# FFN1 over two groups of weight chunks that stay on chip, plain products for one tile pair, and a new order of parts

## The chip, the cores and the metric

The kernel runs on one core of a Trainium2 chip. The metric is the device time of one execution in microseconds. Engines are named as in the profile: PE is TensorE's matmuls and PEld its weight loads, DVE is VectorE, ACT is ScalarE, POOL is GpSimd, SP is SyncE, whose queue issues nearly all DMAs here.

## What is computed

The block takes x (2048 tokens, 512 features), normalizes each token, and computes two branches of the normalized xn. All arithmetic is float32.

```python
xn  = layernorm(x)
q, k, v = split(xn @ wqkv)                     # 32 heads of 16
pq, pk  = q @ w_phi, k @ w_phi                 # per head, 16 x 16
phi = concat(softmax(p), softmax(-p))          # 32 features a head
kv  = phi_k^T v ;  z = sum over tokens of phi_k
o   = (phi_q kv) / (phi_q z + 1e-6)
s   = o @ wo
h   = xn @ w1 + b1                             # 512 -> 1792
g   = silu( mish(h) @ w2 )                     # 1792 -> 512
out = x + s * g
```

## The kernel before, in words

**Tiles.** Tokens are cut into 16 tiles of 128 (t = 0 to 15), the 1792 hidden features into 7 chunks of 256 (b = 0 to 6). A float32 product is made of three products of a high and a low part (`mm3`, line 422): low times high, high times low, high times high. The parts come from `split` (line 442): ACT writes the rounded high part, DVE or POOL subtracts it from the source to give the low part. w_phi is folded into the weights of q and k on chip (`folded`, line 482).

**Fewer products by sums.** k and v of two tiles t and t + 4 are made together by a scheme of seven block products in the place of eight (`kv_a` to `kv_d`, lines 622 to 656). It takes sums and differences of the blocks of the normalized x (`sums_x`, line 545: tiles ts, their parts th and tl) and of the weights (`weights_s`, line 903: four sums ws, their parts in the tile wss). A pair takes 42 products 512 wide where plain ones would take 48. FFN1 uses the same scheme (`ffn1a` to `ffn1d`, lines 812 to 840) on 1024 tokens (half q = 0 or 1) and one chunk b at a time; n = 7q + b counts these units, 0 to 13.

**Parts of the work.** norm (N) loads a tile, normalizes and transposes it and writes its two parts to DRAM (scr), the sums to scrT. q_proj (Q) makes q and parks it in DRAM (qd); q_soft (S) brings it back and makes the softmaxes. kv_acc (A) adds a pair to kv and z; `sums` (z, line 922) finishes them: kvf is written to kvd in DRAM and read back as kvw, which the numerators (num, U, PSUM tiles pn) need. den (D) divides, att_out (O) multiplies with wo. FFN1 brings its half of x back from scr and scrT by `load_g` (L, line 774): 14 transfers of 512 KB into tiles fb0 to fb2 and ft0 to ft3, high and low. `prep1` (P, line 745) loads a chunk of w1, makes its sums and splits it into four tiles (w1ah, w1al, w1sh, w1sl), and writes these to DRAM as w1d; for the second half `again1` (M, line 761) loads the four back as w1b. The hidden values go to DRAM (hd); ffn2 (G, line 842) loads them, applies Mish and multiplies with w2; final (E) applies Silu, multiplies by the attention branch and adds x.

**What sets the order.** The functions only record operations (`Program.call`, line 107). TensorE executes the parts in the order of the table ORDER (line 36), one token a part: Ka0 is `kv_a(0)`, Fa3 is `ffn1a(3)`. For the other engines `Program.simulate` (line 177) plays the program with estimated costs and due times and takes at each point the most urgent operation that is ready; operations written with `either` or `copy` go to whichever of two engines is free. Each engine then executes its list strictly in order, and waits at an instruction whose inputs are missing. SP's queue is one of these lists. Every operation is recorded by line 345, so the profile's groups are told apart by tiles. On chip lie 38 large buffers of 4 KB a partition (`SLOTS`, line 33): one holds a part of a w1 chunk, an fb or ft tile, a normalized tile, and so on; PSUM has 8 banks.

Of the kernel before, what the change touches and what calls it, by code (L numbers as in the profile page):

```python
# [17 lines left out]
P = 128  # L18
# [10 lines left out]
BACK, COLD, DRATE, LANES, SWITCH = 1500, 3400, 300, 8, 300  # L29
# [19 lines left out]
class Op:  # L49
    __slots__ = ("impl", "reads", "writes", "at", "idx", "succ", "ndep", "late", "new", "ready", "start", "eng", "sets", "slack", "open", "soon", "pos", "deps", "lock", "part", "half", "code", "tiles")  # L50


class Program:


    def __init__(self, nc):
        self.eng = {"PE": nc.tensor, "V": nc.vector, "G": nc.gpsimd, "A": nc.scalar, "Q": nc.sync}
        self.ops, self.tag, self.cap, self.pe = [], {}, {}, []
        self.group, self.slack, self.part, self.half = None, SLACK, None, False
# [87 lines left out]
    def links(self):  # L147
# [20 lines left out]
        for o in ops:  # L168
            o.new = []
            o.tiles = {n[0] for n in o.reads | o.writes if n[0] in self.tag}  # L170
            for n in o.tiles:
                self.uses[n] = self.uses.get(n, 0) + 1
                if n not in self.first:
                    self.first[n] = o
                    o.new.append(n)

    def simulate(self, at):
# [15 lines left out]
        free = dict(self.cap)  # L193
# [5 lines left out]
        half = False  # L199
        dma = port = 0  # L200
# [24 lines left out]

        def go(o, e):
            nonlocal aset, dma, port, half, code, fetched
# [23 lines left out]
            for n in o.new:  # L251
                free[self.tag[n]] -= 1
                want[self.tag[n]].remove(n)
            busy[e] = now + dur
            end = now + dur + (200 if e == "PE" else 140)
            if e == "Q":
# [5 lines left out]
                end = max(dma + 1000, now + 2000 + nb / 200)  # L262
# [121 lines left out]
def block_kernel(ctx: ExitStack, tc: tile.TileContext, x, wqkT, wv, phi, wo, w1, b1, w2, out):  # L384
# [124 lines left out]
    scr = [dram.tile([P, 4, 2, KC, P], F32, name=f"scr{g}") for g in range(NG)]  # L509
# [9 lines left out]
    def norm(t):  # L519
# [21 lines left out]
        Q.dma_start(scr[g][:, i], f32(w))  # L541
# [79 lines left out]

    def kv_a(p):
# [46 lines left out]
    def kv_acc(p):  # L669
# [8 lines left out]
        with one():  # L678
# [6 lines left out]
            prog.halves()  # L685
# [22 lines left out]
    def num(n):  # L708
# [3 lines left out]
        with one():  # L712
# [8 lines left out]
            prog.halves()  # L721
# [23 lines left out]
    def prep1(b):  # L745
# [26 lines left out]
    hd, w1d, part = {}, {}, {}  # L772

    def load_g(q):

        def combo(name, src):
            ts = [slot([P, 4, 2, P], f"f{name}{'hl'[u]}{q}", F32R) for u in range(2)]
# [4 lines left out]
        fx[q] = [combo(f"b{n}", lambda u: scr[2 * q + g][:, :, u, 2 * k:2 * k + 2]) for n, g, k in ((0, 0, 0), (1, 0, 1), (2, 1, 1))]  # L782
        fx[q] += [combo(f"t{n}", lambda u: scrT[q][:, :, u, n]) for n in range(4)]
# [101 lines left out]
    w["kv"] = [None] * 7  # L885
    kr, vr, sr = [None] * 2, [None] * 2, [None] * 4

    def weights_k(i):
# [6 lines left out]
        w["kv"][i] = hi, lo  # L895
# [26 lines left out]
    def sums():  # L922
# [16 lines left out]
        for i in range(4):  # L939
# [7 lines left out]
             "Ka": kv_a, "Kb": kv_b, "Kc": kv_c, "Kd": kv_d, "A": kv_acc, "Q": q_proj, "S": q_soft, "D": den, "U": num,  # L947
             "O": att_out, "L": load_g, "P": prep1, "M": again1, "R": prep2,
# [38 lines left out]
```

## Time and profile before

| | |
|---|---|
| median of 3 runs | 527.02 us (526.35 to 529.43) |
| profiled execution, its own time | 527.38 us |
| its span, first to last instruction | 525.6 us |
| mean granted TensorE clock | 0.990 |
| DMA | 128.66 MB, 245 GB/s over the span |
| FFN1's copy of the weights: w1d written, w1b read | 28 and 28 transfers of 384 or 512 KB |

The page gives busy time by engine, then the span in 40 slices (13.1 us each), with the busy share in tenths. A TensorE product 512 wide is listed with 390 to 400 ns, but starts 227 ns after the one before it: they overlap, and a full PE row does not mean that none was late. What is lost is seen by the time between starts, or by idle time listed ahead of an instruction ("idle before", with what ended it). VectorE, ScalarE and GpSimd instructions of a chain that wait on each other show as busy only while they run.

### The profile page before, as it was taken

How to read it: one execution, taken by the hardware profiler on the slowest of the kernel's cores; microseconds unless marked ns; L12 is line 12 of the kernel's file. 1: busy time of each engine (PE TensorE's matmuls, PEld its weight loads, DVE VectorE, ACT ScalarE, POOL GpSimd, SP SyncE). 2: the span in 40 equal slices, each digit the busy share in tenths (PEclk: the TensorE clock that was granted, in tenths of full speed). 3: DMA queues.
4: the chain of work that ended last, by engine and by line, in shares of the span. 5: the costliest groups of instructions: out<-in, count | busy, mean ns of one | idle time of the engine just before them, and what ended most of it. 6: DMA issues, size and time to landing. Idle time of an engine off the chain costs nothing.

```text
span 525.6 us, 8636 instructions
## 1 busy us (share of the span) xinstructions
PE 501.0 (95%) x3204; PEld 409.6 (78%) x3204; DVE 400.7 (76%) x548; ACT 271.8 (52%) x389; POOL 301.5 (57%) x192
## 2 busy tenths in 40 slices
PE   8598989999999899899799999999999999999996
PEld 8486877888888677687677888888888887788885
DVE  5989989989989987889967228889998998323114
ACT  4756665554533534242234245578959759466101
POOL 2988799888989777558310003568977973000000
PEclk9789999999999999999999999999999999999999
DMA  8673867797796966999998377899344734165452
GB/s 305 265 234 135 318 265 279 298 347 265 254 315 217 366 215 252 312 324 392 372 395 263 134 241 255 299 325 401 138 136 127 269 111 161 43 204 156 153 168 80
DMA packets 63945, 128.66 MB, mean 245 GB/s; under 512 B 7456, under 2 KB 23200, under 8 KB 63904
## 3 DMA queue, kind: packets, MB, share of 16 engines
q1 hardware_dynamic: 63760, 127.86, 69.6%
q8 instruction: 25, 0.41, 0.3%
q10 hardware_dynamic: 144, 0.26, 0.1%
q14 instruction: 16, 0.13, 0.1%
HBM read 71.08 MB, written 57.02 MB: 244 GB/s over the span
## 4 chain that ended last, share of the span: by engine, by line
PE 78%; DVE 9%; DMA 7%; ACT 3%; issue 2%; POOL 0%; SPq 0%; DVEq 0%; ACTq 0%
PE y L345 29%; PE fx L345 9%; PE pw L345 8%; PE q L345 7%; PE kx L345 7%; PE fy L345 4%; PE ky L345 4%; PE fz L345 2%; PE pn L345 2%; DMA ft3l<-scrT 1%; DMA w1b<-w1d 1%; DMA qp<-qd 1%; DMA fb2l<-scr 1%; PE kz L345 1%; PE wake L345 1%
## 5 line engine op out<-in xcount | busy, mean ns | idle before, releaser
L345 PE MATMUL q<-wqh,xT 128*128 128x512 f32 x128 | 42.6, 395 | 0.5 <-ACT qs L345 0.3
L345 ACT ACTIVATE r<-r,b1t 128x512 f32<-128x512 f32 x56 | 37.8, 719 | 9.7 <-DMA r<-hd 9.4
L345 DVE TENSOR_TENSOR u<-u,sr 128x512 f32<-128x512 f32 (+1 forms) x13 | 12.6, 974 | 32.5 <-DMA sr<-so 19.6
L345 ACT ACTIVATE so<-pw 128x512 f32<-128x512 f32 x14 | 8.4, 598 | 41.7 <-PE pw L345 41.7
L345 ACT ACT_TABLE_LOAD x21 | 26.9, 1283 | 4.4 <-DMA r<-hd 2.8
L345 PEld LDWEIGHTS q<-wqh,xT 128*128 128x128 f32 x128 | 24.1, 188 | 6.1 <-ACT v L345 0.5
L345 POOL TENSOR_TENSOR u<-u,sr 128x512 f32<-128x512 f32 x4 | 6.0, 1520 | 34.5 <-ACT u L345 34.5
L345 PE MATMUL q<-wql,xT 128*128 128x512 f32 x64 | 25.0, 391 | 0.0
L345 ACT ACTIVATE u<-y 128x512 f32<-128x512 f32 (+1 forms) x17 | 9.4, 573 | 24.9 <-PE y L345 23.7
L345 PE MATMUL kx<-wss,th 128*128 128x512 f32 x64 | 20.8, 408 | 1.3 <-DVE wss L345 1.3
L345 POOL TENSOR_TENSOR a7l<-r,a7h 128x1024 fp32r<-128x1024 f32 x1 | 2.4, 2407 | 31.9 <-ACT a7h L345 31.9
L345 DVE TENSOR_REDUCE tz<-ez 128x64 f32<-128x1024 f32 x16 | 19.1, 1206 | 0.6 <-POOL ez L345 0.6
L345 ACT ACTIVATE hb<-fx 128x512 f32<-128x512 f32 x13 | 7.8, 600 | 22.4 <-PE fx L345 22.4
L345 ACT ACTIVATE ha<-fx 128x512 f32<-128x512 f32 x14 | 8.4, 598 | 20.5 <-PE fx L345 17.5
L345 PE MATMUL kx<-wss,tl 128*128 128x512 f32 x32 | 13.5, 422 | 5.7 <-ACT wss L345 4.3
L345 POOL TENSOR_TENSOR rs<-rs,mhalf 128x1 f32<-128x1 f32 x16 | 10.2, 643 | 14.5 <-DVE rs L345 14.5
L345 POOL TENSOR_TENSOR tl<-ts,th 128x1024 fp32r<-128x1024 f32 x6 | 16.3, 2718 | 2.7 <-issue 2.7
L345 ACT ACTIVATE hc<-fx 128x512 f32<-128x512 f32 x12 | 7.1, 596 | 20.0 <-PE fx L345 20.0
L345 ACT ACTIVATE qs<-q 128x512 f32<-128x512 f32 x16 | 9.5, 596 | 14.5 <-PE q L345 11.4
L345 DVE TENSOR_TENSOR ol<-pn,oh 128x256 fp32r<-128x256 f32 x32 | 11.2, 416 | 6.0 <-ACT oh L345 6.0
L345 PEld LDWEIGHTS kx<-wss,th 128*128 128x128 f32 x64 | 12.4, 196 | 4.2 <-DVE wss L345 1.8
L345 PE MATMUL fy<-fb2h,w1b 128*128 128x512 f32 x32 | 11.3, 394 | 3.1 <-DVE hc L345 3.1
(770 smaller groups left out, 1893.9 us busy)
## 6 DMA issues: line engine op xcount, KB each, us to landing
r<-hd SPq DMA_DIRECT2D x28, 512.0 KB, 5.0
scr<-xT SPq DMA_DIRECT2D x16, 512.0 KB, 3.6
w1b<-w1d SPq DMA_DIRECT2D x14, 512.0 KB, 6.7
w1b<-w1d SPq DMA_DIRECT2D x14, 384.0 KB, 5.8
scrT<-th SPq DMA_DIRECT2D x8, 512.0 KB, 3.1
scrT<-tl SPq DMA_DIRECT2D x8, 512.0 KB, 4.2
qd<-qs SPq DMA_DIRECT2D x16, 256.0 KB, 2.7
qp<-qd SPq DMA_DIRECT2D x16, 256.0 KB, 5.5
```

Source lines behind the costliest of these rows:

```text
L345: getattr(e, m)(*a, **k)
```

## The change

FFN1's seven chunks are worked in two groups, chunks 0 to 3 and chunks 4 to 6 (`GROUPS`). Group one is done for half 0 and then half 1, group two for half 1 and then half 0. A chunk's four weight tiles stay on chip from `prep1` to the last of its two uses; the copy w1d, the reload `again1` and its parts M0 to M6 are gone. In exchange the tiles of x are loaded three times (half 0, half 1, half 0 again: L0, L1, L2) where two loads stood.

Tiles 0 and 4 (pair p = 0) get their k and v by plain products (`k_plain`, `v_plain`: parts K0, K4, V0, V4) in the place of Ka0, Kb0, Kc0 and Kd0; for this the first half of wv is split too. The sums of x of that pair are still made, since FFN1 needs them.

Odd groups of four tiles write only the upper half of the transposed features to scr, the only half that is read. The planner's estimates change (a clock that grows cold again, a later landing of DMAs, two costs for pairs of small products), and the table ORDER is another one: 242 parts.

```diff
-BACK, COLD, DRATE, LANES, SWITCH = 1500, 3400, 300, 8, 300
+BACK, COLD, CHILL, DRATE, LANES, SWITCH, DLAG = 1500, 3400, 3500, 300, 8, (300, 960), 300
...
+PLAIN = (0,)
+GROUPS = ((0, 1, 2, 3), (4, 5, 6))
 ORDER = """
-wv0 wk0 wv1 ws0 N0 N1 wk1 ws1 N4 wq0 N5 Ka0 Kb0 N2 ws2 wq1 Ka1 Kc0 Q2 Ka2 N8 N6 ws3 Kd0 N3 Q5 N7 Q8 Kb1 Kc1 Q4 Ka3 N12
+N0 wv0 wq0 wv1 N1 N4 wk1 V4 wk0 V0 N5 wq1 b1 N8 ws0 Ka1 K0 Q4 Q1 N12 N2 Q0 Ka4 ws2 ws1 N3 Q2 Q8 Kb1 Kc1 Q12 N6 N7 Q3
...
-    scr = [dram.tile([P, 4, 2, KC, P], F32, name=f"scr{g}") for g in range(NG)]
+    scr = [dram.tile([P, 4, 2, KC - g % 2 * 2, P], F32, name=f"scr{g}") for g in range(NG)]
...
-        Q.dma_start(scr[g][:, i], f32(w))
+        Q.dma_start(scr[g][:, i], f32(w)[:, :, g % 2 * 2:])
...
+    def kv_plain(t, n):
+        ps, u = bank([P, D], f"{'kv'[n]}{t}"), (w["k"], w["v"])[n]
+        for i in range(2):
+            with one():
+                for k in (2 * i, 2 * i + 1):
+                    mm3(ps, (xT[t][:, 0, k, :], xT[t][:, 1, k, :]), (u[i][0][:, k % 2], u[i][1][:, k % 2]), k == 0, k == KC - 1)
+        return ps
+
+    def k_plain(t):
+        kp[t] = held(kv_plain(t, 0), f"kp{t}")
+        k_soft(t)
+
+    def v_plain(t):
+        v = vp[t] = alloc("vb", [P, D], f"v{t}")
+        copy(v, kv_plain(t, 1))
...
         w1_[b] = ts
-        w1d[b] = [dram.tile([P, 4, 2 * P], F32, name=f"w1d{b}{i}") for i in range(4)]
-        for i, (d, t) in enumerate(zip(w1d[b], ts)):
-            n = 3 if i < 2 else 4
-            Q.dma_start(d[:, 0:n], f32(t)[:, 0:n])
-
-    def again1(b):
-        w1_[b] = [slot([P, 4, 2 * P], f"w1b{i}{b}", F32R) for i in range(4)]
-        for i, (t, d) in enumerate(zip(w1_[b], w1d[b])):
-            n = 3 if i < 2 else 4
-            Q.dma_start(f32(t)[:, 0:n], d[:, 0:n])
...
+    loads, use = [], {}
+    for i, bs in enumerate(GROUPS):
+        for q in (i % 2, 1 - i % 2):
+            if not loads or loads[-1] != q:
+                loads.append(q)
+            for b in bs:
+                use[q, b] = len(loads) - 1
...
-        xh, xl = fx[q][x]
+        xh, xl = fx[use[q, b]][x]
...
-            w["kv"][2] = split_raw(vr[1], "wv")
+        w["v"][i] = split_raw(vr[i], f"wv{i}")
+        if i:
+            w["kv"][2] = w["v"][1]
```

Three places of the order show the move. The first is TensorE's list where its first use of the summed weights wss stands. In names, kx0 and kz0 are sums of pair 0 in PSUM, wkh and wkl the parts of the folded weight of k, th0 and tl0 those of the sums of x. Before:

```order
L345 MATMUL kz0_206<-wkh1_173,xT0_162 128x512 x2
L345 MATMUL kz0_206<-wkl1_174,xT0_162 128x512
L345 MATMUL kz0_206<-wkh1_173,xT0_162 128x512
L345 MATMUL kx0_205<-wss_157,tl0_188 128x512
L345 MATMUL kx0_205<-wss_157,th0_187 128x512 x2
```

Now plain products stand first, v of tile 4 ahead of all, in two halves by the two halves of wv:

```order
L351 MATMUL wkf11_187<-phit_102,wkT11_146 128x128 x4
L351 MATMUL v4_189<-wv0h_155,xT4_176 128x512
L351 MATMUL v4_189<-wv0l_156,xT4_176 128x512
L351 MATMUL v4_189<-wv0h_155,xT4_176 128x512 x2
L351 MATMUL v4_189<-wv0l_156,xT4_176 128x512
L351 MATMUL v4_189<-wv0h_155,xT4_176 128x512
L351 MATMUL v4_189<-wv1h_163,xT4_176 128x512
L351 MATMUL v4_189<-wv1l_164,xT4_176 128x512
```

Twelve wide products stood ahead of wss; now 120 do, and its first use is pair 1's.

The second place is SP's queue around kvd, the DRAM copy of the finished kv. Before, the w1d copies and w1b reloads stand there (hd are hidden values going out, qp a parked q coming back):

```order
L345 DMA hd11_581<-hc1_580 128x512
L345 DMA qp1_610<-qd1_110 128x512
L345 DMA w1b02_623<-w1d20_338 128x768
L345 DMA w1b12_624<-w1d21_339 128x768
L345 DMA hd01_567<-hd1_582 128x512
L345 DMA hd11_581<-hb1_569 128x512
L345 DMA hd04_591<-ha4_590 128x512
L345 DMA w1d50_606<-w1ah5_602 128x768
L345 DMA w1d42_578<-w1sh4_574 128x1024
L345 DMA w1d43_579<-w1sl4_575 128x1024
L345 DMA kvd_598<-kvf_592 128x256
L345 DMA w1d51_607<-w1al5_603 128x768
```

Now:

```order
L351 DMA qp7_602<-qd7_116 128x512
L351 DMA kvd_592<-kvf_586 128x256
L351 DMA fb2h1_566<-scr3_106 128x4x256
L351 DMA hd13_554<-hc3_553 128x512
L351 DMA hd11_561<-hc1_560 128x512
L351 DMA fb2l1_567<-scr3_106 128x4x256
L351 DMA ft0h1_568<-scrT1_108 128x4x256
L351 DMA ft0l1_569<-scrT1_108 128x4x256
L351 DMA ft1h1_570<-scrT1_108 128x4x256
L351 DMA ft1l1_571<-scrT1_108 128x4x256
L351 DMA ft2h1_572<-scrT1_108 128x4x256
L351 DMA ft2l1_573<-scrT1_108 128x4x256
```

The copies are gone, and most of the second load of x (names that end in 1) stands behind kvd.

The third place is TensorE's list where the first numerators (pn) stand. Before, they follow the first two of unit 13's seven block products, with units 7, 10, 11 and 12 still to be begun:

```order
L345 MATMUL fx13_746<-fb0h1_681,w1b06_698 128x512
L345 MATMUL fz13_747<-fb1h1_683,w1b16_699 128x512
L345 MATMUL fz13_747<-fb1l1_684,w1b06_698 128x512
L345 MATMUL fz13_747<-fb1h1_683,w1b06_698 128x512
L345 MATMUL fz13_747<-fb1h1_683,w1b16_699 128x512
L345 MATMUL fz13_747<-fb1l1_684,w1b06_698 128x512
L345 MATMUL fz13_747<-fb1h1_683,w1b06_698 128x512
L345 MATMUL pn1_0_750<-ph0_618,kvw_599 32x256
```

Now they follow the fifth of unit 5's, with four block products of FFN1 left:

```order
L351 MATMUL fx6_761<-ft2h2_719,w1sh6_683 128x512
L351 MATMUL fx5_738<-ft2h2_719,w1sl5_670 128x512
L351 MATMUL fx5_738<-ft2l2_720,w1sh5_669 128x512
L351 MATMUL fx5_738<-ft2h2_719,w1sh5_669 128x512
L351 MATMUL fx5_738<-ft2h2_719,w1sl5_670 128x512
L351 MATMUL fx5_738<-ft2l2_720,w1sh5_669 128x512
L351 MATMUL fx5_738<-ft2h2_719,w1sh5_669 128x512
L351 MATMUL pn0_0_786<-ph0_601,kvw_593 32x256
```

In all, 1938 wide products become 1944. 504 of them stood ahead of the first FFN1 product, 414 between that and the first numerator, and 1020 behind it; now 522, 576 and 846 do.

More of the change, by code (lines that the diff above doesn't have):

```diff
@@ L49 @@
 class Op:
-    __slots__ = ("impl", "reads", "writes", "at", "idx", "succ", "ndep", "late", "new", "ready", "start", "eng", "sets", "slack", "open", "soon", "pos", "deps", "lock", "part", "half", "code", "tiles")
+    __slots__ = ("impl", "reads", "writes", "at", "idx", "succ", "ndep", "late", "ready", "start", "eng", "sets", "slack", "open", "soon", "pos", "deps", "lock", "part", "half", "code", "tiles")
 class Program:
@@ L58, in __init__ @@
         self.ops, self.tag, self.cap, self.pe = [], {}, {}, []
-        self.group, self.slack, self.part, self.half = None, SLACK, None, False
+        self.group, self.slack, self.part, self.half = None, SLACK, None, 0
     @staticmethod
@@ L100, in add @@
         o.pos, o.part, o.half = len(self.pe), self.part, self.half
-        self.half = False
+        self.half = 0
         o.lock = {e for e, (_, calls) in impl.items() if any(locks(e, m, a) for m, a, k in calls)}
@@ L122, in call, with halves @@
             g[3].extend(s)
-    def halves(self):
-        self.group[0]["PE"][0] += SWITCH
-        self.half = True
+    def halves(self, k):
+        self.group[0]["PE"][0] += SWITCH[k]
+        self.half = SWITCH[k]
     @contextmanager
@@ L168, in links @@
         for o in ops:
-            o.new = []
             o.tiles = {n[0] for n in o.reads | o.writes if n[0] in self.tag}
@@ L174, in links @@
                     self.first[n] = o
-                    o.new.append(n)
     def simulate(self, at):
@@ L192, in simulate @@
             want[self.tag[n]].append(n)
-        free = dict(self.cap)
+        free, held = dict(self.cap), set()
         pe = self.pe
@@ L198, in simulate @@
         aset = 0
-        half = False
-        dma = port = 0
+        half = dma = port = 0
+        warm = last = None
         code, fetched = HEAD, 0
@@ L210, in fits @@
         def fits(o):
-            for t in {self.tag[n] for n in o.new}:
-                mine = [n for n in o.new if self.tag[n] == t]
+            new = o.tiles - held
+            for t in {self.tag[n] for n in new}:
+                mine = [n for n in new if self.tag[n] == t]
                 if t == "ps" and "PE" in o.impl:
@@ L226, in go @@
         def go(o, e):
-            nonlocal aset, dma, port, half, code, fetched
+            nonlocal aset, dma, port, half, code, fetched, warm, last
             dur, calls = o.impl[e]
@@ L233, in go @@
                         aset = s
-            if e == "PE" and now < pe[0].start + COLD if pe[0].start is not None else e == "PE":
-                dur *= 2
             if e == "PE":
+                if last is None or now > last + CHILL:
+                    warm = now + COLD
+                if now < warm:
+                    dur *= 2
                 if half and o.half:
-                    dur -= SWITCH
+                    dur -= o.half
                 half = o.half
@@ L250, in go @@
             o.start, o.eng = now, e
-            for n in o.new:
+            for n in o.tiles - held:
                 free[self.tag[n]] -= 1
                 want[self.tag[n]].remove(n)
+                held.add(n)
             busy[e] = now + dur
+            if e == "PE":
+                last = now + dur
             end = now + dur + (200 if e == "PE" else 140)
@@ L261, in go @@
                 dma = max(dma, now + (1100 if now > 2500 else 1350)) + nb / DRATE
-                end = max(dma + 1000, now + 2000 + nb / 200)
+                end = max(dma + 1000, now + 2000 + nb / 200) + (DLAG if now > 20000 else 0)
                 lanes.append(end)
@@ L283, in simulate @@
                 bad = [o for o in ops if o.start is None][:5]
-                raise RuntimeError(f"no progress at {now}: {[(list(o.impl), o.writes, o.late, o.ready, o.new) for o in bad]} {free}")
+                raise RuntimeError(f"no progress at {now}: {[(list(o.impl), o.writes, o.late, o.ready) for o in bad]} {free}")
             now, kind, i = heapq.heappop(events)
@@ L684, in kv_acc @@
                               start=False, stop=t == NT - 1, skip_group_check=True)
-            prog.halves()
+            prog.halves(0)
     def den(t):
@@ L770, in prep2, with load_g @@
         w2_[b] = split_raw(t, f"w2{b}")
-    hd, w1d, part = {}, {}, {}
-    def load_g(q):
+    hd, part = {}, {}
+    loads, use = [], {}
[5 more added lines that the diff above has]
+                use[q, b] = len(loads) - 1
+    def load_g(i):
+        q = loads[i]
         def combo(name, src):
-            ts = [slot([P, 4, 2, P], f"f{name}{'hl'[u]}{q}", F32R) for u in range(2)]
+            ts = [slot([P, 4, 2, P], f"f{name}{'hl'[u]}{i}", F32R) for u in range(2)]
             for u, t in enumerate(ts):
@@ L780, in combo @@
             return ts
-        fx[q] = [combo(f"b{n}", lambda u: scr[2 * q + g][:, :, u, 2 * k:2 * k + 2]) for n, g, k in ((0, 0, 0), (1, 0, 1), (2, 1, 1))]
-        fx[q] += [combo(f"t{n}", lambda u: scrT[q][:, :, u, n]) for n in range(4)]
+        fx[i] = [combo(f"b{n}", lambda u: scr[2 * q + g][:, :, u, 2 * k:2 * k + 2]) for n, g, k in ((0, 0, 0), (1, 0, 1), (2, 1, 0))]
+        fx[i] += [combo(f"t{n}", lambda u: scrT[q][:, :, u, n]) for n in range(4)]
     def product(ps, n, a, x, first):
@@ L884, in block_kernel @@
     w = {n: [None] * KC for n in "qo"}
-    w["kv"] = [None] * 7
+    w["kv"], w["k"], w["v"] = [None] * 7, [None] * 2, [None] * 2
     kr, vr, sr = [None] * 2, [None] * 2, [None] * 4
@@ L894, in weights_k @@
             copy(kr[i][:, j], ps)
-        w["kv"][i] = hi, lo
+        w["kv"][i] = w["k"][i] = hi, lo
     def weights_v(i):
```

20 lines of the change are left out of this document (10 added, 10 removed).

## The prediction

> **What bounds the kernel now.** I read the page's engine rows and slices first, then the chain that ended last in order of time, then the busy time in stretches, then the groups of TensorE's instructions with idle time before them.
>
> ```profile
> PE 501.0 (95%) x3204; PEld 409.6 (78%) x3204; DVE 400.7 (76%) x548; ACT 271.8 (52%) x389; POOL 301.5 (57%) x192
> PE   8598989999999899899799999999999999999996
> DVE  5989989989989987889967228889998998323114
> PEclk9789999999999999999999999999999999999999
> ```
>
> TensorE is the bound, but its slices are short of full only in the first half, and there VectorE is at eight or nine tenths too. The chain gives the prices and the borders of three stages.
>
> ```profile
> 1.11 5.91 PE wake L345 x26
> 30.99 1.86 PE wqf L345 x16
> 79.50 1.03 PE kvp L345 x64
> 86.20 0.87 PE pt L345 x8
> 157.79 1.58 PE fx L345 x6
> 268.43 2.69 PE pn L345 x116
> 346.45 92.48 PE y L345 x408
> 499.49 22.12 PE y L345 x120
> ```
>
> Columns are start, length and number. A product 512 wide costs 92.48 / 408 = 0.2267 us when nothing holds it. The other prices are 0.116 us for a piece of a fold (1.86 / 16), 0.109 for a transpose, 1.03 for one accumulation of a tile pair. Stage A runs to the first FFN1 product (157.8), B to the first numerator (268.4), C to TensorE's end (499.49 + 22.12 = 521.6).
>
> ```profile
> core 0: 525.6 us, clock 0.990
> 0.00:157.80 157.80, 146.47 (x979) 120.53 (x979) 140.39 (x226) 89.30 (x131) 131.88 (x102) 0.97 0.76 273
> 157.80:268.40 110.60, 101.34 (x617) 80.49 (x620) 97.93 (x132) 38.11 (x58) 75.06 (x47) 1.00 0.89 311
> 268.40:521.60 253.20, 253.20 (x1617) 208.61 (x1616) 161.50 (x189) 144.02 (x200) 94.59 (x44) 1.00 0.59 200
> 521.60:525.60 4.00, 0.00 (x0) 0.00 (x0) 0.86 (x3) 0.38 (x1) 0.00 (x0) 1.00 0.36 131
> ```
>
> The columns are the stretch, its length, busy time of PE, PEld, DVE, ACT and POOL, granted clock, DMA share, GB/s. C is packed: 253.20 of 253.20. So the whole question is what A and B lose beyond their work. Counting in TensorE's order, A holds 504 wide products (114.3 us), the wake products (5.9), 64 pieces of folds (7.4), 64 transposes (7.0) and five accumulations (5.2): 139.8 us. It lasts 157.8 - 1.1 = 156.7, so it loses 16.9. B holds 414 wide products (93.9), three accumulations (3.1) and the two sums of z (2.0, row below): 99.0 of 110.6, so it loses 11.6. The sum of before: 1.1 + 139.8 + 16.9 + 99.0 + 11.6 + 253.2 + 4.0 = 525.6.
>
> **The change, part by part.** The plain products for tiles 0 and 4 take 48 wide products in the place of 42: 6 x 0.2267 = 1.4 us more. The new order has 522 wide products in A, 576 in B (all of FFN1 but its last four block products now stands ahead of the first numerator) and 846 in C. So A's work is 139.8 + 18 x 0.2267 = 143.9, B's is 99.0 + 162 x 0.2267 = 135.7, and C, if it stays packed, lasts 253.2 - 174 x 0.2267 = 213.8. With lead and tail that is 1.1 + 143.9 + 135.7 + 213.8 + 4.0 = 498.5 us, to which the losses of A and B come.
>
> What A loses at its start:
>
> ```profile
> 23.02 0.77 PE L345 MATMUL kx<-wss,tl 128*128 128x512 f32 x1 [4.29 <-ACT wss L345]
> 25.07 1.22 PE L345 MATMUL kx<-wss,th 128*128 128x512 f32 x2 [1.29 <-DVE wss L345]
> 18.40:23.00 4.60, 0.33 (x2) 0.01 (x1) 4.53 (x9) 4.60 (x9) 4.60 (x2) 0.76 0.82 335
> 23.00:25.10 2.10, 0.79 (x2) 0.31 (x2) 2.10 (x3) 0.36 (x1) 2.10 (x2) 0.50 0.98 328
> 25.10:42.00 16.90, 16.90 (x72) 14.12 (x73) 14.39 (x26) 7.73 (x11) 15.09 (x12) 0.83 0.74 233
> 42.00:45.00 3.00, 1.36 (x9) 0.72 (x8) 3.00 (x8) 2.46 (x4) 1.30 (x2) 1.00 0.00 0
> ```
>
> After twelve products TensorE waits 4.29 and 1.29 us for the summed weights wss, and the granted clock falls to 0.50 and stays below full: 16.90 x (1 - 0.83) = 2.9 us more, and some 0.4 on the product at 23.02. That is 8.9 of the 16.9. Two waits for transposes at 42 to 45 add 1.6; 6.4 lie scattered. The new order puts 120 products ahead of the first use of wss where 12 stood, which is 108 x 0.2267 = 24.5 us of cover, and the 8.9 should go. What is late next is the split weight of v.
>
> ```profile
> 4.55 1.11 SPq L345 DMA_DIRECT2D wvr<-wv  x2
> DMA to landing us min/median/max: 6.1/6.4/6.7
> L345 ACT ACTIVATE wvh<-wvr x1: 1077/1077/1077, 16.4 to 16.4; 128x1024 fp32r<-128x1024 f32 x1
> L345 POOL TENSOR_TENSOR wvl<-wvr,wvh x1: 2389/2389/2389, 26.8 to 26.8; 128x1024 fp32r<-128x1024 f32 x1
> L345 ACT ACTIVATE x<-x,nb,rs 128x512 f32<-128x512 f32 x15 | 12.2, 812 | 3.7 <-DVE nb L345 3.6
> L345 DVE TENSOR_TENSOR xT<-pt,xT x4: 679/682/692, 12.5 to 22.0; 128x512 fp32r<-128x512 f32 x4
> ```
>
> The first half of wv is now the fifth load of SP's queue, issued near 3.2 us by the pitch of these issues: 3.2 + 6.4 + 1.1 (ACT) + 2.4 (POOL) = 13.1, and ACT has two normalizations of 0.8 ahead of it that end late, so near 14.4. TensorE's folds and transposes last until about 13 (0.9 for each fold of four, the last two behind tile 4's transposes near 11.2). The low part of the second half is VectorE's instruction 22, behind five of 0.4 to 0.7 us that wait for tile 4, so near 17, which holds the second half of the first plain v for 1.3 us more. v for tile 4 then ends near 18.4, where 13.6 of work is done (5.9 + 3.7 folds + 1.3 transposes + 2.7): 18.4 - 1.1 - 13.6 = 3.7 lost. The transposes of tiles 5 and 8 behind it wait for normalizations that VectorE orders after the splits of wk: 1.7 more by the like waits at 42 to 45. So 5.4 in place of 8.9 + 1.6. For the 6.4 scattered I take 4.4: VectorE has 8 instructions fewer ahead of the first FFN1 sum than before (8 x 140.39 / 226 = 5.0 us) for 4.1 more of TensorE's work. A then loses 9.8; bounds 5 (the scattered ones gone) and 16.9.
>
> In B the groups with idle time before them are these.
>
> ```profile
> L345 PE MATMUL fz<-fb1h,w1b 128*128 128x512 f32 x16 | 5.7, 397 | 0.9 <-DVE hb L345 0.9
> L345 PE MATMUL fx<-ft3h,w1al 128*128 128x512 f32 x12 | 4.9, 409 | 0.7 <-ACT hc L345 0.7
> L345 PE MATMUL fz<-fb1h,w1al 128*128 128x512 f32 x12 | 4.8, 401 | 0.9 <-DVE ha L345 0.9
> L345 PE MATMUL fy<-fb2l,w1sh 128*128 128x512 f32 x12 | 4.8, 399 | 1.7 <-DMA fb2l<-scr 1.7
> L345 PE MATMUL fy<-fb2h,w1b 128*128 128x512 f32 x12 | 4.3, 400 | 3.1 <-DVE hc L345 3.1
> L345 PE MATMUL fx<-ft1h,w1b 128*128 128x512 f32 x12 | 4.3, 399 | 2.0 <-DMA w1b<-w1d 2.0
> ```
>
> They hold 9.3 of the 11.6. The 2.0 goes with the copy w1d and its reload: 56 transfers and 2 x 12.8 MB are gone, 14 of 512 KB (7.3 MB) come in for the third load of x. The reload's row and the load of x are alike in price:
>
> ```profile
> w1b<-w1d SPq DMA_DIRECT2D x14, 512.0 KB, 6.7
> ft1h<-scrT SPq DMA_DIRECT2D x2, 512.0 KB, 6.3
> ```
>
> The third load is hidden where its tiles come free: 10 to 16 us of products lie between the last reader of a tile and the next one's first use, against 6.3 to land. If it were not, each late transfer costs like the 2.0. The 4.9 that VectorE ended shrink, since its share falls: between the two borders stand 154 of its instructions in the place of 121, 33 x 97.93 / 132 = 24.5 us more, so 122.4 for 135.7 of TensorE's work (0.90, before 97.9 for 99.0, 0.99). I take 1.5. The second load of x stands behind kvd in SP's queue:
>
> ```profile
> 194.33 1.98 PE L345 MATMUL pz<-zacc,ones 128*128 128x512 f32 x4
> 199.94 0.32 SPq L345 DMA_DIRECT2D kvd<-kvf  x1
> ```
>
> kvd went out 5.6 us after the last accumulation, which the z sums followed at once. Now two block products of FFN1 (2 x 6 x 0.2267 = 2.7 us) lie between the two, so kvd goes out 2.9 after the z sums begin. Behind it stand six transfers of 512 KB and two of 256 KB (3.7 MB, 11.8 us at the 311 GB/s of stage B) until ft1 has landed, some 2 later. It is first read 13.1 us of products after the z sums: 2.9 + 11.8 + 2 - 13.1 is 3.6 late at that rate, and in time if the queue, with 20 MB less to move, runs a third faster; I take 2. With 2.0 for the rest B loses 5.5; bounds 2 and 11.6.
>
> Sum: 498.5 + 9.8 + 5.5 = 513.8 us of span. The profiled execution took 527.38 around its 525.6, so 1.8 lie outside, and the median of the runs, 527.02, is 0.4 under it: 513.8 + 1.8 - 0.4 = **515.2 us**. A floor from VectorE, which executes in order: its work up to the first numerator is 140.4 - 5.0 + 122.4 = 257.8, with as much idle time as before (17.4 + 12.7) 287.9, where TensorE without losses stands at 1.1 + 143.9 + 135.7 = 280.7. So 7.2 of losses at least unless VectorE idles less. In C it has 400.7 - 9 x 0.74 - 257.8 = 136 left (nine instructions fewer in all) for 213.8, a share of 0.64 as before (162.4 of 253.2), so I cost C's move at nothing; without that cover each late softmax would cost its lateness.
>
> **The rivals.**
> 1. *A cold start.* If TensorE's gap ahead of the first plain v is as long as the 4.29 at 18.7, its clock falls as it did there: 2.9 more, 518.1, once the weight of v is 3 us later than worked out. For it: my 14.4 hangs on one landing time and on ACT's order. Against: I work out gaps of 1.3 us alone. The Trainium skill, "TensorE: Matmul & The Clock Gate", section "HAM oscillation — how this bites in real kernels", warns of idle gaps over about 3.4 us; the 4.29 with the 0.50 behind it agrees, and by that rule gaps of 1.3 us leave the clock alone. No run here shows the border. 0.07.
> 2. *Given back in A.* VectorE and POOL are busy 140.4 and 131.9 of 157.8, and ten of the elementwise operations move to POOL (193 tensor operations in the place of 183), whose split took 2.4. If they pace A whatever the order, it keeps its 16.9 and B loses 8: 523.4, as a time 524.8. Against: the largest wait there names one weight, not a pace. 0.15.
> 3. *More than forecast.* Losses at VectorE's floor, 7.2: 505.7, as a time 507.1. Against: the start alone costs me 5.4. 0.13.
> 4. *Slower: kvd holds the queue.* kvf needs the last accumulation and four VectorE instructions; behind its DMA stand all that is left of the second load, two results that free buffers, and TensorE in order. Every us that kvf is later than in the row goes to the end. From 11.8 us it is slower than before; 16 with the clock's 2.9 gives 534.1. For it: VectorE is as full as before just there. Against: 5.6 was the whole delay then. 0.05.
> 5. *The weights don't fit.* Four chunks hold 16 tiles, two sets of x 28, and there are 38 slots: the second set can be no more than partly ahead. If both later loads show, at 3.4 each (one pair of 512 KB at 311 GB/s), 522.0. 0.07.
>
> **How the numbers follow.** The forecast has 0.53. The range goes down to 506, below the floor of rival 3, and up to 525, which takes in rival 2; half of rival 3, rival 4 and the slower part of rival 2 are left out, some 0.18. A measurement of this kernel tells about 1% (5.3 us) from no change. Faster by more: forecast, rivals 1 and 3, half of 5 and a little of 2, 0.80. Within 1%: 0.15. Slower: rival 4, 0.05.
>
> **What would show it.** Right: wide products run on from about 19 us with no wait for wss over 1 us, and the clock stays at full behind it; FFN1 begins at 1.1 + 143.9 + 9.8 = 155, the first numerator at 296 or so, and from there TensorE has no gap; the packets fall by about 20 MB of the 128.66. Wrong: the first FFN1 product after 160; waits named ft1 or ft0 of some us near 200; a gap behind the first numerator, where less FFN1 work is left to fill in for late softmaxes.

## The result, and the profile after

The changed kernel takes 507.66 us (median of 4 runs, 506.29 to 508.89), the kernel before 526.8 beside it: a ratio of 0.963, with an interval of 0.959 to 0.967. The profiled execution took 507.37 us around a span of 505.4. Its engine rows, slices and transfers:

```profile
PE 495.7 (98%) x3210; PEld 408.4 (81%) x3210; DVE 381.3 (75%) x539; ACT 268.9 (53%) x385; POOL 320.4 (63%) x202
...
PE   8899999999999999999999999999999999999996
...
DVE  4899898989899989989886989894487865214404
...
PEclk9999999999999999999999999999999999999999
...
DMA packets 64296, 108.20 MB, mean 214 GB/s; under 512 B 6784, under 2 KB 31744, under 8 KB 64256
```

TensorE is busy at nine tenths or more in every slice from the third to the last but one, the clock falls in no slice, and 20.46 MB fewer are moved. The borders of the three stages stand in the chain, first FFN1 product, first numerator and TensorE's last group:

```profile
151.06 1.36 PE fx L351 x6
...
287.87 2.68 PE pn L351 x117
...
484.93 16.58 PE y L351 x90
```

The same borders as stretches (length, then busy time of PE, PEld, DVE, ACT, POOL, clock, DMA share, GB/s):

```profile
0.00:151.10 151.10, 146.08 (x997) 121.44 (x998) 131.23 (x218) 86.10 (x128) 130.32 (x98) 1.00 0.60 213
151.10:287.80 136.70, 135.92 (x772) 111.04 (x771) 122.73 (x164) 58.00 (x83) 93.76 (x59) 1.00 0.84 283
287.80:501.50 213.70, 213.69 (x1443) 175.90 (x1442) 126.46 (x157) 124.39 (x174) 96.29 (x47) 1.00 0.50 172
```

With the work that the prediction counted, stage A lost 151.06 - 1.1 - 143.9 = 6.1 us, B 287.87 - 151.06 - 135.7 = 1.1, C took 484.93 + 16.58 - 287.87 = 213.6, and 3.9 follow. The longest of what TensorE still waited for (in total, times, longest):

```profile
PE pt L351 <- ACT x L351: 1.9, 3, 1.1
PE wake L351 <- DVE mhalf L464: 1.1, 1, 1.1
PE v L351 <- DVE wv1l L351: 0.8, 1, 0.8
PE fy L351 <- DMA ft0l<-scrT: 0.8, 1, 0.8
```

There is no wait for wss and none for w1b. The new waits are the two that plain products and the third load of x bring (wv1l and ft0l), 0.8 us each.

### The profile page after: what moved, and what is told of

It reads as the page before. It is cut to its first block, busy times and chain, and to the rows that moved or that the text cites. A ratio compares the mean times of both kernels' runs of the same rounds, so it can differ in the third digit from the quotient of the medians.

```text
span 505.4 us, 8565 instructions
## 1 busy us (share of the span) xinstructions
PE 495.7 (98%) x3210; PEld 408.4 (81%) x3210; DVE 381.3 (75%) x539; ACT 268.9 (53%) x385; POOL 320.4 (63%) x202
## 4 chain that ended last, share of the span: by engine, by line
PE 89%; DVE 4%; DMA 3%; ACT 2%; issue 1%; SPq 0%; ACTq 0%
PE y L351 30%; PE fx L351 14%; PE pw L351 9%; PE fy L351 7%; PE q L351 7%; PE kx L351 7%; PE ky L351 4%; PE fz L351 3%; PE pn L351 2%; DMA ft0l<-scrT 2%; PE kvp L351 2%; PE kz L351 1%; PE pt L351 1%; DVE st L351 1%; DMA x<-x 1%; DMA scr<-xT 1%
## 5 line engine op out<-in xcount | busy, mean ns | idle before, releaser
L351 DVE TENSOR_TENSOR u<-u,sr 128x512 f32<-128x512 f32 (+1 forms) x10 | 10.8, 1078 | 28.8 <-ACT u L351 20.5
L351 POOL TENSOR_TENSOR a26l<-r,a26h 128x1024 fp32r<-128x1024 f32 x1 | 2.4, 2408 | 46.7 <-DMA xx<-x 46.7
L351 ACT ACTIVATE so<-pw 128x512 f32<-128x512 f32 x11 | 6.6, 596 | 29.3 <-PE pw L351 29.3
L351 ACT ACTIVATE ha<-fx 128x512 f32<-128x512 f32 x14 | 8.4, 598 | 18.4 <-PE fx L351 18.4
L351 PE MATMUL kx<-wss,th 128*128 128x512 f32 x56 | 17.3, 390 | 0.0
L351 ACT ACTIVATE hd<-fx 128x512 f32<-128x512 f32 x13 | 7.8, 597 | 16.7 <-PE fx L351 16.7
L351 ACT ACTIVATE qs<-q 128x512 f32<-128x512 f32 x16 | 9.5, 594 | 13.4 <-PE q L351 11.2
L351 POOL TENSOR_TENSOR u<-u,sr 128x512 f32<-128x512 f32 x7 | 11.3, 1636 | 7.2 <-ACT u L351 7.2
L351 ACT ACTIVATE v<-kx 128x512 f32<-128x512 f32 x14 | 8.0, 594 | 14.8 <-PE kx L351 9.2
L351 ACT ACTIVATE x<-x,nb,rs 128x512 f32<-128x512 f32 x15 | 11.8, 809 | 5.5 <-DVE nb L351 3.8
L351 DVE COPY so<-pw 128x512 f32<-128x512 f32 x5 | 3.4, 689 | 14.8 <-PE pw L351 14.8
```

Of the source, the lines that this page charges most:

```text
L351: getattr(e, m)(*a, **k)
```

## Experiments

Two kinds of edit are used. In the first the order of parts is edited and the planner then lays out all engines anew. In the second every instruction stays where it was and a few are added that the planner doesn't see: what stands in prog.pre is issued just ahead of the next operation. The ratios are to the kernel before, run beside each.

| kernel | median us | ratio | interval |
|---|---|---|---|
| b_plain | 541.09 | 1.027 | 1.021 to 1.032 |
| a_shared_q | 525.71 | 0.998 | 0.996 to 1.000 |
| a_oldorder | 565.17 | 1.073 | 1.066 to 1.080 |
| a_copies | 524.26 | 0.995 | 0.992 to 0.998 |
| b_fill | 521.56 | 0.987 | 0.981 to 0.992 |
| a_copies_f | 531.88 | 1.007 | 1.004 to 1.010 |
| a_vector | 524.18 | 0.994 | 0.991 to 0.997 |
| a_kvd | 513.26 | 0.971 | 0.963 to 0.979 |
| t_neither | 516.10 | 0.980 | 0.977 to 0.983 |
| t_plain | 527.58 | 1.001 | 0.999 to 1.004 |
| t_kept | 502.76 | 0.954 | 0.951 to 0.957 |
| t_both | 503.62 | 0.956 | 0.953 to 0.959 |

### One part alone, with an order edited by hand

b_plain is the kernel before with the functions of the plain products and a new head of the order:

```diff
-wv0 wk0 wv1 ws0 N0 N1 wk1 ws1 N4 wq0 N5 Ka0 Kb0 N2 ws2 wq1 Ka1 Kc0 Q2 Ka2 N8 N6 ws3 Kd0 N3 Q5 ...
+N0 wv0 wq0 wv1 N1 N4 wk1 V4 wk0 V0 N5 wq1 N8 ws0 Ka1 K0 Q4 Q1 N2 Q0 Ka2 ws2 ws1 N6 Q2 Q8 K4 ws3 N3 Q5 ...
```

> The kernel before with one part of the change: tiles 0 and 4 get k and v by plain products, wv is split at once, and the order of the first 28 parts is close to the changed one, so that six projections of q stand ahead of the first use of wss. FFN1, its copies and reloads stay. Theory (two separate gains, one at each end): the wait for wss and the low clock behind it go (8.9 us) with most of the 1.6 at the transposes, some 3 to 4 come at wv and the transposes, 1.4 are added by six more products: 526.8 - 10.5 + 3.5 + 1.4 = 521 (519 to 523). Rival 'pace': VectorE and POOL set the pace of this stage whatever its order, and the time is given back before FFN1 begins: 525 to 528. Rival 'new order as a whole': without the rest of the order it brings nothing: 526 or more.

a_shared_q is the changed kernel without plain products:

```diff
-... wk1 V4 wk0 V0 N5 wq1 b1 N8 ws0 Ka1 K0 Q4 Q1 N12 N2 Q0 Ka4 ws2 ws1 N3 Q2 Q8 Kb1 Kc1 ... K4 ... ws3 N13 Kd1
+... wk1 wk0 N5 wq1 b1 N8 ws0 Ka0 Ka1 Q4 Q1 N12 N2 Q0 ws2 ws1 N3 Q2 Q8 Kb0 Kc0 Kb1 Kc1 ... ws3 Kd0 N13 Kd1 Ka4
```

> The changed kernel without its plain products: the first pair shares its products again, but k of tiles 0 and 1 and the projections of q of four tiles stand ahead of the first use of wss, so that cover stays. Theory 'cover, not plain products': the six products more are saved (-1.4), and at the start TensorE waits for the folded weights of k where the plain v stood, 2 to 3 us: 507.7 - 1.4 + 2.5 = 508.8 (507 to 511). Rival 'plain products needed': the wait for wss and the low clock come back, 507.7 + 8.9 - 1.4 = 515 (513 to 518).

a_oldorder is the changed kernel with b_plain's order up to the end of FFN1, its chunks renamed to the two groups and the later loads placed by hand:

```diff
-... P3 L0 S1 Fa0 Fa2 Kd6 Fb0 Fb2 Fc2 Fc0 A5 Fa3 Fd0 ...
+... S6 L0 A4 Fa2 Kd7 Fb2 Kd6 A5 Fc2 S7 Fd2 Fa0 Fa1 Fb1 ...
```

> The changed kernel with the order of before wherever the kept weights allow it: start as in b_plain, stage A and the rows of FFN1 as before with the chunks renamed to the two groups, then the numerators and what follows as changed. Theory (the scheme carries the second gain, the order only places it): stage A as in b_plain, FFN1 with some us of waits for the second load of x, since its place was not tuned: 512 (509 to 516). Rival 'the order is the gain': 518 or more, near what b_plain gives. Rival 'the order is nothing': 508.

All three came out far slower than any theory that named an upper bound. b_plain (541 us) and a_oldorder (565) are met only by the rivals that were open upward ("526 or more", "518 or more"), 15 and 47 us beyond the number named there, and a_shared_q (525.7) by none. The waits lie all over, on normalizations, kp, v, xT and hb. The longest of a_oldorder and of a_shared_q:

```profile
PE fz L351 <- DVE hb L351: 8.5, 1, 8.5
PE ky L351 <- DVE v L351: 7.3, 1, 7.3
PE pt L351 <- ACT x L351: 6.2, 5, 2.8
```

```profile
PE q L351 <- DVE xT L351: 3.6, 2, 2.4
PE pt L351 <- ACT x L351: 3.4, 3, 1.6
PE fy L351 <- DVE ha L351: 3.0, 1, 3.0
```

So these three tell nothing of the two parts. The waits suggest why: an order fits one scheme. TensorE executes in order, and so does each of the engines that feed it, so a part moved by hand can make some VectorE or ACT result late that TensorE needs at once. To tell the parts apart takes either frozen orders or orders made anew for each scheme. Both follow.

### The traffic of the copies

a_copies puts the 28 copies of the combined w1 back into the changed kernel, planned; a_copies_f adds the same with every other instruction in its place, four at a chunk's first row (a row is one chunk on one half of the tokens):

```diff
 def prep1(b):                       # a_copies
     w1_[b] = ts
+    for i, t in enumerate(ts):
+        n = 3 if i < 2 else 4
+        d = dram.tile([P, 4, 2 * P], F32, name=f"w1d{b}{i}")
+        Q.dma_start(d[:, 0:n], f32(t)[:, 0:n])
     def ffn1d(n):                   # a_copies_f: n < 4 or n > 10 is a chunk's first row
         x, y, h = part.pop(n)
+        if n < 4 or n > 10:
+            for i, t in enumerate(w1_[n % NB]):
...
+                prog.pre.append(("Q", "dma_start", (d[:, 0:c], f32(t)[:, 0:c]), {}))
```

> The changed kernel with the 28 copies of the combined w1 to DRAM put back (12.8 MB written, read by nobody): the traffic of the old scheme without its reloads. Theory (the copies cost only where a load that TensorE waits for stands behind them; in the stages before the first numerator the DMA share is 0.60 and 0.84): 507.7 + 1 to 3 = 509.5 (507.5 to 511). Rival 'DMA is the gain': 5.5 MB more in the stretch from FFN1's start to the first numerator, which moves 39.3 MB at 283 GB/s, push it towards the 361 GB/s that was the most in any stretch, and loads come late as before: 515 or more.

> The changed kernel with every instruction in its place on all engines and the 28 copies of the combined w1 to DRAM (12.8 MB) added on SP's queue, four behind the last kind of product of each chunk's first row. In a_copies the planner also moved other work, and 16.6 us came; here only queue and traffic are left. Theory (the planner's moves made most of it): 507.7 + 1 to 4 = 510. Rival 'traffic and queue': 520 or more.

In a_copies, with the planner's moves, the copies cost 16.6 us, as the rival "DMA is the gain" had it. With nothing moved they cost 24, so the rival "traffic and queue" holds. In a_copies_f TensorE's longest waits are for the loads of x (total, times, longest):

```profile
PE fx L354 <- DMA ft1h<-scrT: 6.1, 1, 6.1
PE fx L354 <- DMA ft3h<-scrT: 3.2, 1, 3.2
```

and in the two stretches where they lie the DMA engines have nothing left:

```profile
180.00:220.00 40.00, 30.61 (x234) 23.34 (x233) 30.02 (x45) 11.03 (x17) 18.27 (x12) 0.86 1.00 347
...
270.00:311.70 41.70, 34.70 (x140) 26.76 (x138) 26.95 (x40) 11.22 (x18) 15.11 (x8) 0.96 1.02 373
```

The DMA share is 1.00 and 1.02 there, at 347 and 373 GB/s. The clock falls too (0.86, 0.96). Length less busy time times clock, TensorE loses 13.7 and 8.4 us in the two stretches, and the first numerator starts at 311.8 for 287.9. All 28 copies fall behind FFN1's start here, so this prices 12.8 MB in the fullest stage, not the old scheme, which spread 25.6 MB wider.

### The wait for wss and the clock

b_fill leaves the kernel before in its order and adds ten products ahead of the first use of wss:

```diff
+        if p == 0:
+            prog.pre = [("PE", "matmul", (y, xT[t][:, 0, 0, :], w["kv"][0][0][:, 0]), dict(start=True, stop=True))] * FILL
```

> The kernel before with every instruction in its place and ten products 512 wide more (2.3 us) on TensorE ahead of the first product that reads wss; they write a bank that the next product starts anew. Theory (the low clock behind the wait comes from the length of the gap): the idle gap of 4.29 us shrinks to 2.0, the granted clock stays at full from 25 to 42 us, and the 3.3 us that the low clock cost (2.9 + 0.4) go by 42 us. At 42 two waits of 0.8 for normalizations by ACT stand next; if ACT and VectorE set those times, the gain is given back there: 523.5 if it is kept, 526.5 if it is given back. Rival 'the gap doesn't matter' (the clock falls by time or load): the clock is 0.83 there as before, and 526.5.

521.56 us: 5.7 less than before for work that computes nothing. The same four stretches as in the prediction:

```profile
18.40:23.00 4.60, 3.76 (x17) 2.47 (x15) 4.53 (x8) 4.60 (x9) 4.60 (x2) 1.00 0.82 335
23.00:25.10 2.10, 0.47 (x2) 0.15 (x2) 2.10 (x3) 0.33 (x1) 2.10 (x2) 1.00 1.02 333
25.10:42.00 16.90, 16.27 (x84) 13.41 (x85) 16.60 (x34) 10.82 (x17) 16.90 (x14) 1.00 0.71 237
42.00:45.00 3.00, 2.79 (x15) 2.11 (x13) 2.69 (x5) 2.13 (x5) 3.00 (x4) 1.00 0.45 145
```

The wait for wss still ends at 25.1, but the gap of 4.29 us ahead of it is filled but for waits of 0.5 and 0.4, the clock stays at 1.00 where it was 0.50 and 0.83, and TensorE executes 84 instructions from 25.1 to 42 where it did 72. The gain is kept, and the waits at 42 to 45 shrink as well (2.79 busy where 1.36 was). So the low clock was on the path, and the gain, 4 to 10 us by its interval, is no less than the 3.3 us that the prediction gave it.

### VectorE's room and the queue behind kvd

Both leave the changed kernel in its place:

```diff
         plus(h, z)                  # a_vector, in ffn1a
+        prog.pre = [("V", "tensor_copy", (h, h), {})] * 2
         kvd = dram.tile(...)        # a_kvd
+        kve, kvx = dram.tile([P, NC * 32], F32, name="kve"), kvf.rearrange("p g a b d -> p (g a b d)")
+        prog.pre = [("Q", "dma_start", (kve, kvx), {}), ("Q", "dma_start", (kvx, kve), {})]
```

> The changed kernel with every instruction in its place and two more copies 128x512 in place on VectorE per row of FFN1 (28 in all, about 0.34 us each by the like of them, 26 of them or 8.7 us ahead of the first numerator). Theory 'floor' of the prediction (VectorE executes in order with as much idle time as before, so its work up to the first numerator sets it): the first numerator moves by about all of it, 287.8 to 296, and the time is 507.7 + 8 = 516. Rival 'slack' (VectorE's idle time of some 32 us there is spare): under 2 us more, 509.

The copies are far dearer on the mean than expected. Their busy time and mean ns, then the shortest, median and longest, and four rows of the timeline (start and length in us; ha<-ha is the copy):

```profile
L349 DVE COPY ha<-ha 128x512 f32<-128x512 f32 x28 | 27.8, 993 | 0.5
...
L349 DVE COPY ha<-ha x28: 364/486/2514, 160.6 to 301.4; 128x512 f32<-128x512 f32 x28
...
160.60 1.94 POOL L354 TENSOR_TENSOR k15e<-k15e,k15r 128x1024 f32<-128x1024 f32 x1
162.49 2.03 POOL L354 TENSOR_TENSOR w1al<-w1a,w1ah 128x768 fp32r<-128x768 f32 x1
...
160.64 4.16 DVE L349 COPY ha<-ha 128x512 f32<-128x512 f32 x2
...
191.50 0.88 DVE L349 COPY ha<-ha 128x512 f32<-128x512 f32 x2
```

The four pairs of copies with no operation of GpSimd beside them take 0.82 to 0.88 us, as the one at 191.50 does, and that is not far from the size expected. The ten that overlap one take 1.00 to 4.16, as the one at 160.64 does. So the size expected was wrong where GpSimd works beside VectorE, but the question has its answer. Up to the first numerator, of the changed kernel and of a_vector:

```profile
0.00:287.80 287.80, 282.00 (x1768) 232.47 (x1769) 253.96 (x381) 144.10 (x211) 224.09 (x156) 1.00 0.71 246
```

```profile
0.00:303.00 303.00, 286.52 (x1768) 233.81 (x1768) 271.31 (x408) 146.09 (x214) 223.26 (x156) 0.99 0.67 232
```

VectorE's busy time is 271.31 - 253.96 = 17.4 us more, and the numerator comes at 303.09, 303.09 - 287.87 = 15.2 later; its idle time stays near 32 us (33.8, 31.7). "Slack" falls. "Floor" holds for the 17.4 of busy time, not for the 27.8 of the copies: one other instruction of 2.1 comes later here, and the rest took some 8 less than in the changed kernel, where k14e<-k14m,kp, for one, is listed with 2877 ns for 689 here. So the changed kernel has some room there, far less than the 32 us that VectorE stands idle.

> The changed kernel with every instruction in its place and two small transfers more on SP's queue just ahead of kvd (kvf to DRAM and back, 128 KB each), so that the queue stands for about 5 us until the second has landed; no engine but SP has more to do. ft1h and ft1l were issued at 194.0 and 194.7 and first read at 205.0 and 205.2, so with some 8 us to land they had 2 to 3 us of room. Theory of the prediction's step (what stands behind kvd is late by the delay less the room): a wait of 2 to 3 us named ft1 near 205 and 510. Rival 'every us shows': 512.7. Rival 'hidden' (the queue catches up, since its issues waited for free tiles anyway): 508.

kvd went out at 194.09 where it had at 188.22, 5.9 later, and the transfers behind it followed:

```profile
194.09 0.32 SPq L354 DMA_DIRECT2D kvd<-kvf  x1
...
198.75 0.62 SPq L354 DMA_DIRECT2D ft1h<-scrT  x1
199.47 1.59 SPq L354 DMA_DIRECT2D ft1l<-scrT  x1
```

ft1h is 4.7 later than in the changed kernel, TensorE waited 1.6 and 0.9 for ft1h and ft1l, as the delay less the room says, and then ran 3.5 us at a clock of 0.65, 1.2 more. The span is 510.4, 5.0 over the changed kernel's; in the runs' medians 5.6, with wide intervals. "Hidden" falls. The wait named is that of the first theory, and the time is near the second's, since the clock and the later loads add to it.

### Four kernels with orders made anew

The order of each was searched by moves and swaps of parts, kept where the changed kernel's planner put the end earlier, with the same effort for all. "Kept" is FFN1 in two groups, "plain" the plain products. The heads of the four orders, the parts ahead of the first use of wss (Kb):

```diff
 t_neither
+N8 N12 wk1 wk0 wv0 N1 wq1 wv1 ws0 N2 N0 ws1 wq0 N4 Ka0 ws3 Q8 Ka2 ws2 Kb0
 t_plain
+wv1 wv0 N0 N3 wk1 V0 ws0 wk0 N8 N4 N2 wq1 ws1 wq0 N6 N1 Q0 Q4 N5 Ka1 Q6 N12 Q8 ws2 N11 K0 Ka2 Kb1
 t_kept
+wq1 wv0 wk0 N8 wq0 N1 N5 wk1 N9 ws2 Q8 N0 wv1 Q9 Ka1 Q5 N12 N4 Q0 N13 Q12 N2 Q1 Q13 ws0 Ka0 Q2 Q4 ws1 Kb0
 t_both
+wv1 N0 wv0 ws0 wq0 wq1 N9 N4 Q0 N3 Q9 V4 wk0 V0 N1 Q4 N13 wk1 N2 N5 Q3 Q5 Q2 ws1 Ka1 N8 N7 K4 N12 N6 ws2 Kb1
```

> Four kernels with an order searched anew for each, the same search for all (moves and swaps of parts, judged by the changed kernel's own planner), so that no scheme suffers from an order made for another. This one has neither part of the change: products of the first pair shared, w1 copied to DRAM and read back. Theory 'both parts' (as in the prediction, start and FFN1 each give about half): 523, with the plain products 513 to 516, with the kept weights 514 to 516, with both 506. Theory 'kept weights' (in these orders the cover for wss needs no plain products, and the gain is that of the copies and reloads that go): 517 for this one and for the one with plain products, 507 for the two with kept weights. Theory 'order alone': all four within 3 us of each other.

> Plain products for the first pair, w1 copied and read back, order searched anew. 'Both parts': 513 to 516, well under t_neither. 'Kept weights': as t_neither, 517, perhaps 1.4 above it for the six products more. 'Order alone': as the other three.

> Weights kept in two groups, first pair's products shared, order searched anew. 'Both parts': 514 to 516, since the wait for wss is back. 'Kept weights': 507, no wait for wss over 1 us. 'Order alone': as the other three.

> The changed kernel with its order searched on from where it was. 'Both parts' and 'kept weights': 506 to 508, since its losses were 7 us and the start alone has 4 of them that hang on the first loads. A gain of over 3 us would say that the changed kernel's order was far from done.

t_kept is the fastest of all: 502.76 us, a ratio whose interval lies under that of the changed kernel. It has no plain products. 132 wide products, nine projections of q and two shared k's, stand ahead of its first use of wss at 50.4, and TensorE's whole list of waits is this:

```profile
PE wake L351 <- DVE mhalf L464: 1.1, 1, 1.1
PE q L351 <- DVE wkl L351: 0.9, 1, 0.9
PE pt L351 <- ACT x L351: 0.6, 1, 0.6
```

t_both, with both parts, is 0.9 us slower, each of its six runs above each of t_kept's, so the plain products bring nothing in these two orders; it is some 4 us under the changed kernel, whose order was not done. t_neither, with neither part, is 11 us faster than before by its order and the changed planner. t_plain, from the same search, is not faster than before at all. To see where, I take what TensorE lost in a stretch, its length less busy time times granted clock (summed over pieces of it; the first 60 us hold 1.1 ahead of TensorE's first instruction in each). The first 60 us of the kernel before, t_neither and t_kept:

```profile
0.00:60.00 60.00, 50.33 (x251) 42.25 (x252) 50.74 (x97) 38.22 (x58) 46.05 (x44) 0.91 0.71 254
```

```profile
0.00:60.00 60.00, 51.92 (x261) 44.49 (x262) 49.72 (x96) 38.69 (x59) 43.89 (x42) 0.94 0.77 283
```

```profile
0.00:60.00 60.00, 57.33 (x303) 49.33 (x304) 48.41 (x97) 41.27 (x64) 40.24 (x40) 1.00 0.78 290
```

and the 70 us up to 310 of t_plain, where the reload of w1 is late:

```profile
240.00:310.00 70.00, 64.10 (x497) 50.36 (x496) 42.76 (x67) 20.51 (x41) 20.67 (x11) 0.93 0.74 255
```

| | before | after | t_neither | t_plain | t_kept | t_both |
|---|---|---|---|---|---|---|
| lost, 0 to 60 us | 14.2 | 5.0 | 11.2 | 10.1 | 2.7 | 4.3 |
| lost, 60 to 310 us | 10.9 | 0.8 | 2.9 | 15.2 | 0.1 | 0.0 |

Read along the rows: from 60 to 310 us the three kernels with kept weights lose under 1 us, those with copies 3 to 15. In the first 60 us it is not the plain products that part them (t_kept 2.7, t_plain 10.1) but the order. "Both parts" falls for the plain products, "order alone" falls for the kept weights, and "kept weights" holds with limits: it had t_plain at 517, and the 13.3 us between t_neither and t_kept are more than that part, since 8.5 of them lie in the first 60 us. That kept weights made the better start possible isn't shown; it may be the search, which was made once for each kernel and left t_plain with late reloads. The kernels with copies also write the whole of scr, 2.1 MB more, so that small part of the change counts here with the kept weights. What plain products are worth beside copies stays open, since the order of t_plain failed elsewhere.

## Why the prediction was right, and where it wasn't

The side and the range were right: 515.2 forecast, 507.66 measured, within 506 to 525. It lies 1.7 us from the range's lower end, and nearest to rival 3 (507.1), which had a chance of 0.13. Term by term, in the span (forecast, measured):

- **The work** of the stages held: C 213.8 and 213.6, tail 4.0 and 3.9. With these and losses of 7.2 in A and B the sum gives 505.4, the measured span. All but 0.3 of the miss of 8.4 lies in the two losses.
- **A's loss: 9.8, measured 6.1.** The wait for wss and the low clock went, as said. The wait at wv came where it was put and a little earlier; rows of TensorE, start and length:

```profile
13.25 0.47 PE L351 MATMUL v<-wv0h,xT 128*128 128x512 f32 x1 [0.40 <-DVE xT L351]
...
16.29 0.49 PE L351 MATMUL v<-wv1l,xT 128*128 128x512 f32 x1 [0.82 <-DVE wv1l L351]
...
17.55 0.83 PE L351 MATMUL wkf<-phit,wkT 128*128 128x128 f32 x6
```

v of tile 4 ended at 17.55 for 18.4, so 2.9 were lost for 3.7; the transposes of tiles 5 and 8 lost 1.0 for 1.7; the scattered rest, 4.4 in the sum, was 2.2. This last is the term of A that was most mis-sized. It was scaled from VectorE's instruction count; what is left of it lies for about half at a transpose and a projection of q near 43.7 and 44.7, and from 60 us to FFN1 TensorE loses nothing. That the old scatter had to stay in a new order was assumed, and the kernels with orders made anew (lost from 0 to 60 us: 2.7 to 11.2) show that it follows the order.
- **B's loss: 5.5, measured 1.1.** Three entries: the waits that VectorE ended, 1.5 forecast, are gone; the second load of x behind kvd, 2, was in time; the rest, 2, was 1.1, most of it the third load of x (0.8 at ft0l), which the sum had at nothing. The step on kvd failed in its first number: it took over from the row of before that kvd goes out 5.6 us after the last accumulation. It went out at 188.22, some 1.3 behind the last one (186.25 + 0.63) and ahead of the sums of z. With the delay put back by hand (a_kvd) the wait came as worked out, so the mechanism was right and the delay was not.
- **The copies were priced too low.** The sum took off only the 2.0 that was named w1b. a_copies_f shows, in the new order, that TensorE's loads of x stand behind whatever else the queue and the DMA engines carry there: the relief can lie in every load, not only in the one wait with its name. How much of it the old order had is not measured.
- **The floor from VectorE** gave 287.9 for the first numerator, and it came at 287.87. That it agrees to a tenth is chance: VectorE's work was 254.0 for 257.8, its idle time 33.8 for 30.1, and of TensorE's 7.2 of losses A's 6.1 came in the first 60 us, while from 60 to 310 no wait on VectorE stands in the list. VectorE is near the limit (a_vector: 17.4 more of busy time, 15.2 later), but it isn't shown to have set the first numerator here. The sum stood 8 us above this floor on waits added up one by one, and more than half of that sum did not come.
- **The plain products** gave cover, as worked out, and their 1.4 is part of the work that held. What the prediction did not ask is whether the cover needs them: t_kept has it without.

Of the rivals, the cold start did not come (clock 1.00), A gave nothing back, kvd did not hold the queue, and neither later load of x showed at 3.4. Whether the new order or the two parts made the gain was not among the rivals, and it should have been: with neither part t_neither gains 11 us over the kernel before, with kept weights the same search gains 24. How the changed kernel's own 19 divide is not measured.

## What to carry to other kernels

Where all engines execute in order by one plan, a scheme and its order are one thing: judge a part by orders made anew for each variant, or add to a frozen order, since a hand edit measures the damage to the plan. One search for each variant leaves its luck in the difference. Ahead of a late operand any independent work will do as cover, a projection that is due anyway before products that cost extra. Price a removed copy by the whole stage's transfers when the DMA share there is near 0.9, not by the one wait that has its name.

## What the runs showed of the hardware

The clock falls at shorter waits than the 4.29 us of the prediction. In t_neither a wait of 2.35 us was enough; TensorE's row with its wait, and the stretch behind it (the clock is the third number from the end):

```profile
17.35 1.11 PE L351 MATMUL pt<-ident,x 128*128 128x128 f32 x4 [2.35 <-ACT wkr L351]
```

```profile
17.40:21.00 3.60, 3.60 (x19) 3.60 (x20) 2.97 (x5) 2.78 (x6) 2.44 (x2) 0.57 0.85 341
```

In t_plain one of 2.41 was not:

```profile
234.43 0.50 PE L351 MATMUL fz<-fb1h,w1b 128*128 128x512 f32 x1 [2.41 <-DVE hb L351]
```

```profile
234.30:238.00 3.70, 3.57 (x16) 2.95 (x17) 3.70 (x9) 0.62 (x2) 1.94 (x1) 1.00 1.06 363
```

Nor was one of 2.83 us early in t_plain, whose stretch from 8.4 to 12 us has a clock of 1.00. And in a_kvd two waits of 1.6 and 0.9 close together lowered it to 0.65: TensorE was busy 1.51 of 4 us ahead of that.

```profile
204.50:208.50 4.00, 1.51 (x5) 0.73 (x4) 4.00 (x5) 0.69 (x1) 2.91 (x2) 0.88 1.08 381
208.50:212.00 3.50, 3.50 (x12) 2.79 (x11) 2.65 (x4) 0.60 (x1) 2.82 (x2) 0.65 1.09 384
```

So the length of a single gap doesn't decide. The Trainium skill, "TensorE: Matmul & The Clock Gate", section "HAM oscillation — how this bites in real kernels", sets the border at idle gaps over about 3.4 us; in t_neither 2.35 did it, and the measurement decides. Where exactly the border lies, and whether it is a share of a stretch, these runs leave open.

A copy 128x512 in place on VectorE took from 364 to 2514 ns in a_vector, 993 on the mean, against 689 for copies of the same shape out of PSUM (so<-pw) in the same profile. Of the pairs, the four without an operation of GpSimd beside them took 0.82 to 0.88 us, the ten with one 1.00 to 4.16. So VectorE's busy time holds more than its work, and not only idle time shows that it waits. The expectation of 0.34 fits the shortest, not the mean.
